# Linear attention and an MLP in one kernel: the attention in sub-chunks of 64 tokens instead of 128

## The chip, the cores and the metric

The kernel runs on one core of one Trainium2 chip. The metric is device time in microseconds (us). The kernel before takes 658.77 us, the median of 3 runs (658.64 to 660.05). Traces come from one profiled execution, whose own time is given with it.

Names: PE is TensorE (PEld its weight loads), DVE VectorE, ACT ScalarE, POOL GpSimd, SP SyncE. All products are in float32; in the records each such matmul stands as two weight loads and two matmul records.

## The reference

B = 4 batches, H = 8 heads, S = 768 tokens, D = 64; per head a decay lam between 0.97 and 0.99.

```python
# Linear attention and an MLP in one kernel: the attention in sub-chunks of 64 tokens instead of 128
intra = (qb @ kb.T * Dmask) @ vb            # Dmask[i, j] = lam ** (i - j) for i >= j, else 0
inter = (qb * lam ** (pos + 1)) @ kv_state
out[block] = intra + inter
kv_state = lam ** 64 * kv_state + (kb * lam ** (63 - pos)).T @ vb
...
x = out as (B*S, H*D)                       # 3072 x 512
h = x @ w_in                                # w_in 512 x 2048
g = h - tanh(h)
result = g @ w_out                          # w_out 2048 x 512
```

The block length does not change the result of the attention: a block of 128 with the mask and the powers of 128 tokens gives the same sum.

## The kernel before

The tokens are worked in 6 groups `g` of 128 tokens of all four batches (512 columns). Heads go in pairs: `p` is the pair (4 of them), `j` the head in it, and head j lies on partitions 64 j to 64 j + 63. Each group goes through the attention, through `h` (the function `up` and its relatives; products split in seven and, from group 3 on, again in seven, in the manner of Strassen), through `g - tanh`, and through `down`, `down_twice` (products with w_out, also split).

The attention of a group comes in two halves of two batches, `bs` = (0, 1) and (2, 3). `attention(g)` (L433) lists the pieces of each half, and the main loop places them between the products by calls of `run`:

- `att_transpose` (L315): q and k to head dimension by token, `qt` and `kt`. In groups 0 and 1 by PE (L328) and ACT (L330); from group 2 on by DVE (L335) from small blocks that SP loads in the right order (`load_blocks`, tiles q_blk and k_blk, seven buffers). `qd` = qt times the powers `fwd` (L334, DVE).
- `att_scores` (L337): `sp` = kt x qt, 16 matmuls per half with 64 rows and 128 columns on half of the array each (L344); then DVE multiplies each of four banks with `mask` into `ss` (L349).
- `att_out` (L394): 16 matmuls state x qd on quarters of the array (L410), 16 of v x ss on halves (L416), all in two banks `op`; ACT copies each bank of 512 columns to `xt` (L420).
- `att_state` (L369): 16 matmuls k x v with the decayed k (L385), in one bank `kv`. In groups 1 and 2 DVE multiplies the state and adds kv (L389, L390); from group 3 on ACT puts the scaled state into the bank first (four copies, L378) and copies the bank back (L392). The last group has no state.
- `att_sums` (L423): sums and differences of xt on DVE, for the split products.

The decay of k (times lam^(127-pos)) is one DVE operation per batch in groups 1 and 2 (`att_decay`, L352, within `att_state`), and 8 ACT copies with a scale per batch from group 3 on (`decays`, L361), spread over the steps of the group before it in the stream (iteration g decays group g + 1).

The order is set in three ways. The loop from L1020 on writes out the order of the pieces: in iteration g, the first half of the attention of g + 1 comes after `every(down(g, 2))` (L1055, the products `plain` of L756), then `down` or `down_twice` number 4, then the transposes of the second half, number 5, its scores, number 6, the rest of the second half, and number 7. For group 1 the list `turns` (L967) does this between the plain products of group 0 (L874), where ACT and DVE also round the weights (L283 to L288) and form sums of them (L259 to L262). `early_pieces` (L1099) does the transposes and scores of half 0 of group g + 2 inside the inner steps (L611) of group g + 1. Instructions wrapped in `tied(...)` or `keep_in_program_order` keep the order in which they are written; others may be moved by the scheduler within their engine's stream. And buffers decide: the PSUM tag "att" is a ring of four banks shared by tp, sp, op, kv and some product banks; the natural k tiles have three buffers, so that the k load of batch 3 waits for the kv of half 0 (`load_natural`, L125), and on SP's queue the next group's q_blk and k_blk stand behind it.

The products fetch their weights by POOL's queue: `wb` from `factors`, `fine` and `fine_in` (L709 to L715) through a ring of eight.

Of the kernel before, what the change touches and what calls it, by code (L numbers as in the profile page):

```python
# [18 lines left out]
BLK = 128  # L19
# [5 lines left out]
def kernel(  # L25
# [69 lines left out]
    mask = const.tile([128, 2, NP, BLK], F32)  # L95
    for j in range(2):
        for p in range(NP):
            h = 2 * p + j
            nc.vector.tensor_tensor_scan(out=mask[:, j, p, :], data0=lam_all[:, h:h + 1].to_broadcast([128, BLK]),
                                         data1=ident, initial=0.0, op0=AL.mult, op1=AL.add)  # L100

    fwd = const.tile([128, NP, BLK], F32)

    def powers():
        for j in range(2):
            tc.keep_in_program_order(nc.vector.tensor_copy(
                fwd[ts(j, 64), :, 0], lam_all.rearrange("s (p j) -> s j p", j=2)[ts(j, 64), j, :]))
        m = 1
        while m < BLK:
            tc.keep_in_program_order(nc.vector.tensor_tensor(  # L110
                fwd[:, :, m:2 * m], fwd[:, :, 0:m], fwd[:, :, m - 1:m].to_broadcast([128, NP, m]), op=AL.mult))
            m *= 2


    bwd = mask.rearrange("s j p i -> s p j i")[:, :, :, BLK - 1:BLK].to_broadcast([128, NP, 2, D])

    lam_blk = fwd[:, :, BLK - 1:BLK][:, None, :, :].to_broadcast([128, 2, NP, D])
# [9 lines left out]
    def load_natural(g, b, names):  # L127
        for name, src, bufs in (("q", q, 2), ("k", k, 3), ("v", v, 4)):
            if name in names:
                x = (qpool if name == "q" else io).tile([128, H, D], F32, name=f"{name}_nat", tag=name, bufs=bufs)  # L130
                op = nc.sync.dma_start(out=x, in_=src[b, :, ts(g, BLK), :].rearrange("h s d -> s h d"))
                tc.keep_in_program_order(op)
                raw[g, b][name] = x
# [12 lines left out]
    def load(n):  # L146

        while at["loaded"] < min(n, len(chunks)):  # L150
            g, b = chunks[at["loaded"]]
            if g < GB:
                raw[g, b] = {}
                load_natural(g, b, "qk")
                for x in (b - 1, b) if b % 2 else ():
                    load_natural(g, x, "v")
                at["loaded"] += 1
                continue
            for b in range(B):
                raw[g, b] = {}  # L160
            nat = "kv" if g < NG - 1 else "v"

            first = (0, 1, 2) if g == GB else ()
            for b in first:
                load_natural(g, b, nat)
            for b in range(B - 1):
                load_blocks(g, b, "qk")
            load_blocks(g, 3, "q")
            for b in (0, 1):
                if b not in first:  # L170
                    load_natural(g, b, nat)
            load_blocks(g, 3, "k")
            for b in (2, 3):
                if b not in first:
                    load_natural(g, b, nat)
            at["loaded"] += B
# [133 lines left out]
    state = const.tile([128, B, NP, D], F32)  # L310
# [4 lines left out]
    def att_transpose(g, bs):  # L315
        for b in bs:
# [15 lines left out]
            if g > 0:  # L332
                qd = work.tile([128, NP, BLK], F32, name="qd", tag="qd")
                nc.vector.tensor_tensor(qd, qt, fwd, op=AL.mult)  # L334
            tr[g, b] = (qt, kt, qd)  # L335

    def att_scores(g, bs):  # L337
        for b in bs:
            qt, kt, _ = tr[g, b]

            sp = [bank("sp", "att", 4).rearrange("s (p i) -> s p i", p=NP) for _ in range(2)]
            for p in range(NP):
                for j in range(2):
                    tied(g != GI, nc.tensor.matmul(out=sp[j][:, p, :], lhsT=kt[ts(j, 64), p, :],  # L344
                                                            rhs=qt[ts(j, 64), p, :], start=p == 0, stop=True,
                                                            skip_group_check=True))
            ss = work.tile([128, 2, NP, BLK], F32, name="ss", tag="ss")
            for j in range(2):
                tied(g == 0, nc.vector.tensor_tensor(ss[:, j], sp[j], mask[:, j], op=AL.mult))  # L349
            sc[g, b] = ss  # L350

    def att_decay(g, b):  # L352
        kp = raw[g, b]["k"].rearrange("s (p j) d -> s p j d", j=2)
        tied(g != 1, nc.vector.tensor_tensor(kp, kp, bwd, op=AL.mult))

    def decays(g, bs):

        for b in bs if g < NG - 1 else ():
            for h in range(H):
                k_h = raw[g, b]["k"][:, h, :]  # L360
                tc.keep_in_program_order(nc.scalar.activation(  # L361
                    k_h, k_h, AF.Copy, scale=mask[:, h % 2, h // 2, BLK - 1:BLK]))
# [6 lines left out]
    def att_state(g, bs):  # L369
        if g == NG - 1:  # L370
            return

        kv = bank("kv", "att", 4).rearrange("d (b p e) -> d b p e", b=2, p=NP)
        st = state[:, bs[0]:bs[0] + 2]
        filled = g > GI
        if filled:
            for p in range(NP):
                nc.scalar.activation(kv[:, :, p], st[:, :, p], AF.Copy, scale=fwd[:, p, BLK - 1:BLK])  # L378
        for n, b in enumerate(bs):
            kd, vn = raw[g, b]["k"], raw[g, b]["v"]  # L380
            if 0 < g <= GI:
                att_decay(g, b)
            for p in range(NP):
                for j in range(2):
                    tied(g == 0, nc.tensor.matmul(out=kv[ts(j, 64), n, p, :], lhsT=kd[:, 2 * p + j, :],  # L385
                                                  rhs=vn[:, 2 * p + j, :], start=not filled and n == 0 and p == 0,
                                                  stop=True, skip_group_check=True))
        if 0 < g <= GI:
            nc.vector.tensor_tensor(st, st, lam_blk, op=AL.mult)  # L389
            nc.vector.tensor_tensor(st, st, kv, op=AL.add)  # L390
        else:
            tied(g == 0, nc.scalar.activation(st, kv, AF.Copy))  # L392

    def att_out(g, bs):  # L394
# [4 lines left out]

        def dst(n, p, j):  # L400
            return ops[p // 2][ts(j if p < 2 else 1 - j, 64), p % 2, n, :]


        if g > 0:
            for n, b in enumerate(bs):
                for p in (0, 1):
                    for j in range(2):
                        r = ts(j, 64)
                        for pp in (p, p + 2):
                            nc.tensor.matmul(out=dst(n, pp, j), lhsT=state[r, b, pp, :], rhs=tr[g, b][2][r, pp, :],  # L410
                                             start=n == 0 and p == 0, stop=False, skip_group_check=True)
        for n, b in enumerate(bs):
            ss, vn = sc.pop((g, b)), raw[g, b]["v"]
            for p in range(NP):
                for j in range(2):
                    tied(g == 0, nc.tensor.matmul(out=dst(n, p, j), lhsT=vn[:, 2 * p + j, :], rhs=ss[:, j, p, :],  # L416
                                                  start=g == 0 and n == 0 and p % 2 == 0,
                                                  stop=n == 1 and p % 2 == 1, skip_group_check=True))
        for x in range(2):
            tied(g == 0, nc.scalar.activation(  # L420
                xt[g, half][:, 2 * x:2 * x + 2, :].rearrange("d p (b s) -> d p b s", b=2), ops[x], AF.Copy))

# [10 lines left out]
    def attention(g):  # L433
        pieces = [[(fn, g, bs) for fn in (att_transpose, att_scores, att_out, att_state)] for bs in ((0, 1), (2, 3))]
# [302 lines left out]
    def down(g, n):  # L737
# [14 lines left out]
        for u in range(NU):  # L752
            wb = piece(g, n, u)
            for m in range(2):
                for kt in range(2):
                    nc.tensor.matmul(out=t[:, m, :], lhsT=a[:, u, kt, ts(m, 128)], rhs=wb[:, kt, :],  # L756
                                     start=first and u == 0 and m == 0 and kt == 0, stop=u == NU - 1 and kt == 1,
                                     skip_group_check=True)
# [42 lines left out]
    def down_twice(g, n, zw):  # L801
# [5 lines left out]
        for x, a, dst, keep in ((1, a11, y, o[:, 0:128]), (2, a12, zw[:, 0:128], None), (6, s2, y, o[:, 128:256]),  # L807
# [3 lines left out]
            for u in range(NU):  # L811
                nc.tensor.matmul(out=dst, lhsT=a[:, u, :], rhs=wb[:, ts(u, 128)], start=x in (1, 2) and u == 0,  # L812
                                 stop=u == NU - 1, skip_group_check=True)
# [50 lines left out]
    def up_plain(u, cs):  # L864
# [5 lines left out]
        for i in range(KI):  # L870
            for c in cs:
                a, t = divmod(c - 11, 10)
                for m in range(2):
                    tied(u == 0, nc.tensor.matmul(  # L874
# [19 lines left out]
    def down_first(kt, ns):  # L894

        u, m = divmod(kt, 2)
        for n in ns:
# [4 lines left out]
            for r in range(2):  # L902
                nc.tensor.matmul(out=acc[n][:, r, :], lhsT=a[:, ts(r, 128)], rhs=b, start=kt == 0 and r == 0,  # L903
                                 stop=kt == KH - 1, skip_group_check=True)
# [29 lines left out]
    for b in (0, 1):  # L934
# [33 lines left out]
             (3, 11, 0, p0[1:2]), (3, 21, 1, p0[2:4]), (2, 12, 1, ()), (2, 22, 1, p1[0:1]), (3, 12, 1, p1[1:2]),  # L968
# [18 lines left out]
    run(p1[2:4])  # L987
    weights(NU * KI + 6)
    run(p1[4:])
    for kt in range(KH):  # L990
        down_first(kt, (1, 2))
        if kt + 1 < KH:
# [27 lines left out]
    for g in range(1, NG):  # L1020
        last = g == NG - 1
        (p0, p1), step = ahead, 0
        for u in range(NU):
            if g < GI:
# [12 lines left out]
                if u > 1:  # L1037
                    run(p0[u - 2:u - 1])
# [14 lines left out]
        if twice(g, 4):  # L1053
            sums_twice(g, 4)
        every(down(g, 2))  # L1055
        run(p0[2:])
        sums_twice(g, 5)
        zw = ("w", "z") if g >= GI else ("z", "w")
        every(down_twice(g, 4, zw[0]) if twice(g, 4) else down(g, 4))
# [14 lines left out]
        run(p1[1:2])  # L1074
# [11 lines left out]
        run(p1[2:])  # L1086
# [4 lines left out]
        every(down_twice(g, 7, zw[1]) if twice(g, 7) else down(g, 7))  # L1091
# [70 lines left out]
```

## Time and profile before

| | |
|---|---|
| median of 3 runs | 658.77 us (658.64 to 660.05) |
| the profiled execution | 658.55 us, span 656.8 us, granted clock 1.00 |
| PE busy | 647.6 us, 99% of the span |
| DVE, ACT, POOL busy | 480.6, 244.3, 234.1 us (73%, 37%, 36%) |
| DMA | 140.68 MB, 214 GB/s on average |
| scores, L344 | 384 records of 279 ns |
| inter L410, intra L416 | 320 records of 275 ns; 384 of 276 ns |
| kv, L385 | 320 records of 223 ns |
| xt L420, decays L361, L378 (ACT) | 24 of 596 ns, 64 of 337 ns, 16 of 370 ns |
| ss L349 (DVE) | 48 of 684 ns |

A record's time is its latency; matmuls overlap, so the length of a block of them is read from the starts, or from the chain of waits, which merges consecutive instructions of one line. A group's line gives: line, engine, operation, output and inputs by the program's names, the part of the array and the shape, the count, then busy us, mean ns, and the idle time of the engine just before with what ended most of it.

### The profile page before, as it was taken

Reading aid. Unit: us, or ns where it says so; the run is one execution under the profiler, and the core shown is the slowest. Engines: PE = TensorE matmul, PEld = TensorE weight load, DVE = VectorE, ACT = ScalarE, POOL = GpSimd, SP = SyncE. Lnnn points to the kernel's source line nnn. Section 1 sums busy time; section 2 is a strip of 40 time slices with the busy share of each in tenths; the row PEclk is TensorE's granted clock in tenths of the full one; section 3 lists DMA queues with packets and bytes.
Section 4 is the critical chain, followed back from the end, with each engine's and each line's share of the span. In section 5 each row is a group of like instructions: output and inputs, shape, how many; then the busy total and the mean of one; then the engine's idle time right before and its main releaser. Section 6 shows DMA issues by size and latency. Waiting matters only on the chain.

```text
span 656.8 us, 13884 instructions
## 1 busy us (share of the span) xinstructions
PE 647.6 (99%) x5160; PEld 596.4 (91%) x5160; DVE 480.6 (73%) x929; ACT 244.3 (37%) x502; POOL 234.1 (36%) x400
## 2 busy tenths in 40 slices
PE   7899999999999999999999999999999999999998
PEld 6788888888888999998999998899998899998897
DVE  4577886745788889569866578987567987457963
ACT  3897825503221111246341235533333322333310
POOL 0000535735432355220454521256411246621261
PEclk9999999999999999999999999999999999999999
DMA  9989988969665898874899877599956277942394
GB/s 211 232 238 246 302 287 232 332 168 256 187 159 145 226 288 259 259 183 111 217 301 278 221 181 200 130 283 269 294 133 149 94 241 249 251 144 66 85 306 155
DMA packets 167699, 140.68 MB, mean 214 GB/s; under 512 B 134800, under 2 KB 137488, under 8 KB 167632
## 3 DMA queue, kind: packets, MB, share of 16 engines
q0 software_dynamic: 33376, 106.19, 51.0%
q1 hardware_dynamic: 134112, 33.59, 25.2%
q8 instruction: 41, 0.67, 0.4%
q14 instruction: 26, 0.21, 0.1%
q10 hardware_dynamic: 144, 0.00, 0.0%
HBM read 111.42 MB, written 28.31 MB: 213 GB/s over the span
## 4 chain that ended last, share of the span: by engine, by line
PE 59%; DMA 1%; issue 1%; POOL 0%; DVE 0%; POOLq 0%
PE plain L756 11%; PE y L611 10%; PE y L812 9%; PE zw L812 7%; PE z L611 5%; PE y L533 4%; PE zs L533 4%; PE w L611 3%; PE sp L344 2%; PE op L416 2%; PE end L858 1%; PE op L410 1%; DMA wb<-fine_in 1%; PE kv L385 1%; POOL wb L709 0%
## 5 line engine op out<-in xcount | busy, mean ns | idle before, releaser
L712 POOL DMA_DIRECT2D wb<-fine x133 | 73.8, 555 | 155.2 <-PE plain L756 103.4
L756 PE MATMUL plain<-wb,g 128*128 128x256 f32 x416 | 94.9, 380 | 0.0
L756 PEld LDWEIGHTS plain<-wb,g 128*128 128x128 f32 x416 | 78.0, 190 | 10.3
L715 POOL DMA_DIRECT2D wb<-factors x64 | 34.5, 540 | 70.9 <-PE z L611 51.1
L874 PE MATMUL h<-xt,w 128*128 128x256 f32 x256 | 57.6, 382 | 2.2 <-DVE w L288 2.0
L815 ACT ACTIVATE q<-y 128x128 f32<-128x128 f32 x76 | 21.1, 278 | 96.5 <-PE y L812 95.1
L874 PEld LDWEIGHTS h<-xt,w 128*128 128x128 f32 x256 | 47.8, 190 | 9.4 <-DVE w L288 2.0
L709 POOL DMA_DIRECT2D wb<-fine_in x60 | 35.6, 625 | 32.0 <-PE y L611 6.5
L812 PE MATMUL y<-wb,g 128*128 128x128 f32 x336 | 44.8, 278 | 0.0
L514 ACT ACTIVATE th<-g 128x512 f32<-128x512 f32 x48 | 29.4, 627 | 34.2 <-DVE g L539 34.0
L812 PEld LDWEIGHTS y<-wb,g 128*128 128x128 f32 x336 | 40.7, 192 | 1.1 <-issue 0.3
L602 ACT ACTIVATE g<-y 128x512 f32<-128x512 f32 x24 | 14.3, 597 | 63.6 <-PE y L611 63.6
L349 DVE TENSOR_TENSOR ss<-sp,mask 128x512 f32<-128x512 f32 x48 | 30.3, 684 | 7.6 <-PE sp L344 7.6
L903 PE MATMUL acc<-wt,g 128*128 128x256 f32 x144 | 32.7, 380 | 0.0
L515 DVE TENSOR_TENSOR g<-g,th 128x512 f32<-128x512 f32 x48 | 31.9, 685 | 0.4
L611 PE MATMUL z<-tt,wb 128*128 128x128 f32 x256 | 31.9, 275 | 0.0
L903 PEld LDWEIGHTS acc<-wt,g 128*128 128x128 f32 x144 | 27.2, 190 | 3.9 <-DVE g L910 0.2
L533 PE MATMUL y<-xt,w 128*128 128x256 f32 x128 | 30.3, 379 | 0.0
L533 PE MATMUL zs<-xt,ws 128*128 128x256 f32 x128 | 30.2, 379 | 0.0
L611 PEld LDWEIGHTS z<-tt,wb 128*128 128x128 f32 x256 | 30.2, 192 | 0.0
L812 PE MATMUL zw<-wb,g 128*128 128x128 f32 x224 | 29.6, 275 | 0.0
L284 ACT ACTIVATE r<-raw 128x512 int16<-128x512 uint32 x32 | 25.1, 784 | 7.0 <-DMA raw<-in_moe_w_out_dram 4.0
(224 smaller groups left out, 1484.0 us busy)
## 6 DMA issues: line engine op xcount, KB each, us to landing
wb<-fine POOLq DMA_DIRECT2D x133, 256.0 KB, 4.0
wb<-factors POOLq DMA_DIRECT2D x64, 256.0 KB, 4.3
wb<-fine_in POOLq DMA_DIRECT2D x60, 256.0 KB, 5.0
v_nat<-in_v_dram SPq DMA_DIRECT2D x24, 256.0 KB, 5.0
raw<-in_moe_w_out_dram POOLq DMA_DIRECT2D x12, 512.0 KB, 5.4
k_nat<-in_k_dram SPq DMA_DIRECT2D x20, 256.0 KB, 4.7
out_dram<-q POOLq DMA_DIRECT2D x20, 256.0 KB, 4.2
fine<-wt POOLq DMA_DIRECT2D x17, 256.0 KB, 4.2
```

Source lines behind the costliest of these rows:

```text
L349: tied(g == 0, nc.vector.tensor_tensor(ss[:, j], sp[j], mask[:, j], op=AL.mult))
L514: tied(held, nc.scalar.activation(th, src, AF.Tanh))
L515: nc.vector.tensor_tensor(dst(c), src, th, op=AL.subtract)
L533: nc.tensor.matmul(out=t[:, m, :], lhsT=wt[:, kt, ts(m, 128)], rhs=x[:, kt, :], start=False, stop=kt == 1, skip_group_check=True)
L611: nc.tensor.matmul(out=dst[:, ts(u, 128)], lhsT=a, rhs=b, start=(x in (1, 5) or x == 2 and not filled) and u == 0, stop=True, skip_group_c ...
L709: nc.gpsimd.dma_start(out=t.rearrange("p m c -> p (m c)"), in_=fine_in[INNER.index(n_[1]), (5, 6, 3).index(x_)].rearrange("p u c -> p (u c)"))
L712: nc.gpsimd.dma_start(out=t.rearrange("p m c -> p (m c)"), in_=fine[TWICE.index(n_), SUB.index(x_)].rearrange("p u c -> p (u c)"))
L715: nc.gpsimd.dma_start(out=t, in_=factors[XAT[FACT[n_][1]]][:, 2 * x_:2 * x_ + 2, :])
L756: nc.tensor.matmul(out=t[:, m, :], lhsT=a[:, u, kt, ts(m, 128)], rhs=wb[:, kt, :], start=first and u == 0 and m == 0 and kt == 0, stop=u = ...
L812: nc.tensor.matmul(out=dst, lhsT=a[:, u, :], rhs=wb[:, ts(u, 128)], start=x in (1, 2) and u == 0, stop=u == NU - 1, skip_group_check=True)
L874: tied(u == 0, nc.tensor.matmul(out=hm[c][:, m, :], lhsT=w1[u][:, i, a, ts(m, 128)], rhs=xt[0, t][:, i, :], start=m == 0 and i == 0, stop= ...
L903: nc.tensor.matmul(out=acc[n][:, r, :], lhsT=a[:, ts(r, 128)], rhs=b, start=kt == 0 and r == 0, stop=kt == KH - 1, skip_group_check=True)
```

## The change

From group 1 on, a group of 128 tokens is worked as two sub-chunks `a` of 64 tokens. Group 0 stays as it was, with masks of its own (`whole`, in the pool of output tiles).

- Scores: only the two diagonal blocks of 64 x 64 are formed, 32 matmuls of 64 x 64 x 64 per half, on four quarters of the array, both batches in two banks; two mask products instead of four.
- kv: 32 matmuls with 64 rows per half (one bank per sub-chunk). In the last group 16, for the first sub-chunk alone, which needs k loads (64 rows) and decays that there were not.
- State: three buffers that rotate, `states(g)` = old, mid, new. mid = lam^64 old (four ACT copies), mid += kv of sub-chunk 0 (DVE), new = lam^64 mid + kv of sub-chunk 1 (four DVE operations).
- Output: `att_inter`, 32 matmuls on quarters into four banks of "att", old for sub-chunk 0 and mid for sub-chunk 1; a small ACT copy `seen` of the last bank; `att_intra`, 32 matmuls on quarters into the same banks; xt in four copies of 256 columns. Between inter and intra stands one step of a product, which `held` ties to the order written.
- Order: `att_state` now comes right after the scores in half 1, and before `down(g, 2)` in half 0 of groups 3 to 5. The decays of groups 1 and 2 move into `att_transpose`. `powers` gets four ACT copies of masks and one step less of `fwd`.

```diff
     def att_scores(g, bs):
+        if g > 0:
+            sp = [bank("sp", "att", 4).rearrange("s (n p i) -> s n p i", n=2, p=NP) for _ in range(2)]
...
+                        for a in range(2):
+                            cols = ts(a, HALF)
+                            tied(g != GI, nc.tensor.matmul(
+                                out=sp[j][ts(a, 64), n, p, :], lhsT=kt[ts(j, 64), p, cols], rhs=qt[ts(j, 64), p, cols],
+                                start=n == 0 and p == 0, stop=True, skip_group_check=True))
...
     def att_state(g, bs):
...
+        old, mid, new = (x[:, pair_] for x in states(g))
+        subs = (0, 1) if g < NG - 1 else (0,)
+        kv = [bank("kv", "att", 4).rearrange("d (b p e) -> d b p e", b=2, p=NP) for _ in subs]
+        for p in range(NP):
+            nc.scalar.activation(mid[:, :, p], old[:, :, p], AF.Copy, scale=fwd[:, p, HALF - 1:HALF])
...
+                    for a in subs:
+                        nc.tensor.matmul(out=kv[a][ts(j, 64), n, p, :], lhsT=kd[ts(a, 64), 2 * p + j, :],
+                                         rhs=vn[ts(a, 64), 2 * p + j, :], start=n == 0 and p == 0, stop=True,
+                                         skip_group_check=True)
+        nc.vector.tensor_tensor(mid, mid, kv[0], op=AL.add)
+        for p in range(NP) if g < NG - 1 else ():
+            nc.vector.scalar_tensor_tensor(out=new[:, :, p], in0=mid[:, :, p], scalar=fwd[:, p, HALF - 1:HALF],
+                                           in1=kv[1][:, :, p], op0=AL.mult, op1=AL.add)
...
+    def att_inter(g, bs):
+        st = states(g)
+        open_[g] = {(x, a): bank("op", "att", 4)[:, 0:256].rearrange("d (p b s) -> d p b s", p=2, b=2)
+                    for a in range(2) for x in range(2)}
...
+                            tc.keep_in_program_order(nc.tensor.matmul(
+                                out=corner(g, x, a, p, n, j), lhsT=st[a][r, b, p + 2 * x, :],
+                                rhs=tr[g, b][2][r, p + 2 * x, ts(a, HALF)], start=n == 0 and p == 0, stop=False,
+                                skip_group_check=True))
+        nc.scalar.activation(seen, open_[g][1, 1][:, :, :, 0], AF.Copy)
+        held["yes"] = True
+
+    def att_intra(g, bs):
+        held["yes"] = False
...
+                            tc.keep_in_program_order(nc.tensor.matmul(
+                                out=corner(g, x, a, p, n, j), lhsT=vn[ts(a, 64), h, :],
+                                rhs=ss[ts(a, 64), j, n, p + 2 * x, :], start=False, stop=n == 1 and p == 1,
+                                skip_group_check=True))
+        for (x, a), t in open_.pop(g).items():
+            nc.scalar.activation(xt[g, half][:, 2 * x:2 * x + 2, :].rearrange("d p (b a s) -> d p a b s", b=2, a=2)[
+                :, :, a], t, AF.Copy)
...
+        if g >= GI:
+            run(p0[2:3])
         every(down(g, 2))
-        run(p0[2:])
+        run(p0[3:4])
         sums_twice(g, 5)
...
+        p4 = down_twice(g, 4, zw[0]) if twice(g, 4) else down(g, 4)
+        next(p4)
+        run(p0[4:])
+        every(p4)
...
-        run(p1[1:2])
+        run(p1[1:3])
...
-        run(p1[2:])
+        run(p1[3:4])
+        p7 = down_twice(g, 7, zw[1]) if twice(g, 7) else down(g, 7)
+        next(p7)
+        run(p1[4:])
```

In the lines of the changed kernel, L431 are the copies for mid, L440 the add to mid, L442 the products for new, L485 is `seen`, L505 the xt copies, L481 inter and L500 intra; its roundings are L291 to L296.

## The prediction

> **What bounds the kernel now.** I read the shares of busy time first, then the slices, the chain that ended last, and the groups by shape.
>
> ```profile
> PE 647.6 (99%) x5160; PEld 596.4 (91%) x5160; DVE 480.6 (73%) x929; ACT 244.3 (37%) x502; POOL 234.1 (36%) x400
> ...
> PE   7899999999999999999999999999999999999998
> ...
> PEclk9999999999999999999999999999999999999999
> ```
>
> PE is busy 99% of the span and in every slice after the second; the granted clock is 1.00 throughout. No other engine has a stage of its own. In the view of waits PE waits 6.2 us in all, almost all of it before 30 us. So time taken out of PE's stream comes off the end, unless PE then waits for something that its own length covers today.
>
> The chain of waits around one half of group 3 shows what the attention costs in that stream:
>
> ```profile
> 310.92 4.96 PE plain L756 x23
> 315.88 1.03 PE op L410 x32
> 316.91 1.90 PE op L416 x32
> 318.81 0.93 PE kv L385 x32
> 319.74 1.09 PE y L812 x8
> ```
>
> Columns: start, length, what. Each float32 matmul is two records (x32 is 16 matmuls). The three blocks take 3.86 us; the scores have a stretch of their own, earlier (273.55, 1.99 us, x32). Groups by shape give the forms:
>
> ```profile
> L344 PE MATMUL sp<-qt,kt 64*128 64x128 f32 x384 | 25.2, 279 | 1.4 <-ACT kt L330 1.4
> L416 PE MATMUL op<-ss,v_nat 128*64 128x128 f32 x384 | 23.6, 276 | 0.0
> L385 PE MATMUL kv<-v_nat,k_nat 128*64 128x64 f32 x320 | 11.3, 223 | 0.2 <-PE op L416 0.2
> L410 PE MATMUL op<-qd,state 64*64 64x128 f32 x320 | 11.0, 275 | 0.0
> ```
>
> 128*64 is the part of the array, 64x128 the moving operand. Only L410 uses quarters today; only L385 has 64 columns.
>
> **Rounds.** In the records' starts, matmuls on different parts of the array begin 7 ns apart and then the next round follows: L344 two tiles each 112 ns, L410 four tiles each 109 ns, both with 128 columns; L385 two tiles each 58.5 ns with 64 columns (16 rounds x 58.5 = 0.94, the 0.93 of the chain). So a round's length goes by its columns, and four tiles fit where two do. What no row shows is four tiles with 64 columns. [...]
>
> **What PE saves.** A new block is 32 matmuls, 64 records, in 16 rounds of four. At L385's round that is 0.94 us; entering and leaving the tile mode costs about 0.29 in L344 (2.08 with its entry, less 16 x 0.112), and L410's first round was some 0.05 longer: I take 0.32, so 1.26 a block. Scores and kv, now side by side, enter once: 2.22. A half costs 2.22 + 2 x 1.26 = 4.74. Before it cost 1.99 + 3.86 and twice 0.09 of entry, 6.03. Saved: 1.29 a half.
>
> Three halves get less. In the new order of PE's instructions the kv of half 0 in groups 3 to 5 is not in one piece: 24 matmuls, a full-array product, 8 more (group 3: scores alone 1.26, kv 1.59, saving 0.66); 24/4/4 in group 4 (0.2); 12/3/1 in group 5, whose kv (first sub-chunk only) is new work: before, a half without kv was 5.10; now it loses 0.84. Half 1 of group 5 wins 0.36. Sum: four halves of groups 1 and 2 5.16; group 3 1.95; group 4 1.49; group 5 -0.48: **8.1 us** off PE. Group 0 is as before.
>
> **What the other engines pay.** DVE: a half's four mask products of 128x512 (684 ns; 0.60 start to start) become two; the two state products (0.68 each) become one add and four small ones (at 0.20 to 0.29 each, by 128x128 rows); DVE is 73% busy and some 3 us shorter in all, at no gain by itself. ACT: four extra mask copies of 64x256 (0.38 estimated between 0.28 for 128x128 and 0.60 for 128x512), four copies of 128x128 with a scale for mid per half (L378: 370 ns, 0.395 apart) where groups 1 and 2 had none, one tiny copy `seen`, xt in four pieces of 256 columns instead of two of 512 (1.09 becomes some 1.5), 32 more decays in group 5 (L361: 337 ns, 0.24 to 0.27 apart, 8 us). ACT is 37% busy, so only its place in the order matters. SP: the q and k copies of the next group stand behind the k load that waits for kv of half 0; that wait now ends some 10 us earlier, so they start earlier; the transposes on DVE that read them come earlier too, but their data was in by about 238 against 239.5. The four extra k loads (64 rows, 128 KB each) go into a queue that no PE wait names after 30 us. I cost both at nothing, up to 3 us (DVE's whole wait for q_blk today).
>
> **New waits on PE**, where the saved time is given back:
>
> 1. Group 1, 57 to 100 us, where DVE and ACT are busiest. Inter needs mid and new, which need kv. Four copies for mid and two of the masks stand in ACT's queue before the roundings (L283 to L285); DVE's L288, which waits for them (it started at 69.67), comes some 1.3 later, about 71.0, and L440 and four L442 stand behind it: 71.0 + 0.6 + 0.6 + 0.33 + 0.2 x 4, less what moves up, is about 72.9. Inter is due at 71.05: 1.8 us. In half 1 the same gives 1.05 (95.05 against 94.0), and transposes that wait for the four xt copies behind roundings give 0.45. Together 3.3; nothing if ACT's idle time (0.80 at 65.37) takes up the shift, 6 if DVE's queue does not move up.
> 2. kv of half 0 in groups 3 to 5 now precedes `down(g, 2)`, seven us of `plain`. It waits for the last decays on ACT:
>
> ```profile
> 308.81 7.07 PE L756 MATMUL plain<-wb,g 128*128 128x256 f32 x32
> ...
> 311.27 1.05 ACT L361 ACTIVATE k_nat<-k_nat,mask 128x64 f32<-128x64 f32 x4
> ```
>
>    The last four end 3.5 us after PE has come to this product (3.8 a group later). The first 24 matmuls and the products between cover all but 0.97, 0.6 and 0.4: 2.0. Ends: 0 if ACT gets there as PE slows, 7 if the pieces wait in turn.
> 3. Intra waits for `seen`. In ACT's queue that stands behind four mid copies (1.6 us), and one of these behind the inter that still reads the buffer; the filler between inter and intra is four y products, 0.89. Some 0.6 is left in three halves (group 3 half 0, group 4 both): 1.8; where the filler is four plain products (1.73) nothing is. Ends: 0 and 4.
>
> Sum of waits 7.1. Covered, as far as I see: new of group 2 half 0 (208.9 against 210.3) and group 3 (317.5 against 318.3); in half 1 6.25 us of products lie between. xt is later by 2 us at most, with 4 to 6 to spare. The profiled run is 658.55 (span 656.8 and 1.75 around it), 0.2 under the median of 658.77. 658.55 - 8.1 + 7.1 = 657.5, and 0.2 for the median: **657.7**.
>
> **Rivals.**
>
> A, the waits do not come: PE's products slide, ACT keeps ahead. 658.77 - 8.1 - 0.8 (two waits of 0.38 for fine_in that the shift may remove) gives 650. For it: ACT is idle 63% of the span. Against: each wait has an instruction named in the new order that stands before it.
>
> B, quarters with 64 columns are not fed fast enough, and the kernel is slower. The new rate is one matmul record per 14.6 ns, each with a weight load. The highest mean rate that any row shows is 27 to 29 ns (L410: 109/4; L385: 58.5/2). The bursts of 7 ns speak against a limit, but a burst may come out of a queue that was filled while the array was busy. At 27 ns a block takes 64 x 0.027 + 0.32 = 2.05, 0.79 more; there are 39 such blocks: +31, less the gain, about 682. The point from which it decides: 1.0 us of waits is left as gain, and 39 blocks x 16 rounds eat it at 1.6 ns more per round; at 20 ns a record it is 658 + 13 = 671. [...]
>
> C, the same mechanisms as in the forecast, but at the upper ends: group 1 at 6, kv at 4 and `seen` at 3 make 13 against 8.1: 663.5.
>
> D, the change does not do what it says: kv pieces split so that nothing is saved in groups 3 to 5, 655 to 658; inside the forecast's range.
>
> **Chances.** Forecast (655 to 661) 0.50, A 0.10, B 0.18, C 0.22. Within the forecast, with 657.7 near the bound, faster 0.5, same 0.28, slower 0.22. A measurement of this kernel tells 0.2% (1.3 us) from no change. Faster: 0.25 + 0.10 + a little of D, 0.37. Same: 0.14 and a little of C, 0.15. Slower: 0.11 + 0.18 + 0.22, less that, 0.48. The range goes from 649.5 (A) to 670 (C and the mild part of B), and leaves the hard form of B out.
>
> **What would show it.** Right: blocks of 64 records lasting 1.2 to 1.3 us; PE gaps near 72, 95, 310 and ahead of intra in groups 3 and 4, summing to some 7 us. B would show as rounds of 100 ns and more, without gaps. A would show 1.26 blocks and none of the gaps. Wrong if DVE, with the smaller products, delays the g tiles that `down` reads, which I cost at nothing.

## The result and the profile after

The changed kernel takes 662.28 us, the median of 5 runs (660.94 to 663.63), against 658.64 us before; the ratio is 1.0053 (95% interval 1.0032 to 1.0075). It is slower by 3.6 us, where no change or a little less (657.7) was forecast. Its profiled execution took 660.94 us (span 659.2), the lowest of the five, so the trace accounts for 2.4 of the 3.6 us. Its mean granted clock is 0.995; of the other four, one has 0.995 (662.28), one 0.997 (662.67) and two 1.000 (661.53 and 663.63).

The page, shares of busy time and granted clock by slices:

```profile
PE 643.5 (98%) x6440; PEld 588.0 (89%) x6440; DVE 477.4 (72%) x946; ACT 260.1 (39%) x588; POOL 234.1 (36%) x400
...
PEclk9999989999999999899999999999999999999999
```

PE is busy for 4.1 us less and the span is 2.4 us longer: PE waits. And the clock row has two 8s that were not there.

The groups by shape, for the four products of the attention:

```profile
L437 PE MATMUL kv<-v_nat,k_nat 64*64 64x64 f32 x576 | 13.3, 220 | 0.9 <-ACT k_nat L404 0.9
L500 PE MATMUL op<-ss,v_nat 64*64 64x64 f32 x640 | 11.9, 221 | 0.3 <-issue 0.3
L481 PE MATMUL op<-qd,state 64*64 64x64 f32 x640 | 11.9, 221 | 0.4 <-DVE state L442 0.4
L362 PE MATMUL sp<-qt,kt 64*64 64x64 f32 x640 | 11.6, 221 | 0.0
```

All of them run on quarters with 64 columns, and each block of 64 records takes 0.98 to 1.09 us by the records' starts where it waits for nothing. The quarters are fed.

The view of waits for PE:

```profile
PE tp L340 <- ACT xt L505: 2.1, 1, 2.1
PE z L696 <- DMA wb<-fine_in: 2.1, 1, 2.1
...
PE kv L437 <- ACT k_nat L404: 0.9, 2, 0.6
PE z L553 <- DVE g L579: 0.7, 1, 0.7
PE op L481 <- DVE state L442: 0.4, 1, 0.4
PE op L500 <- issue: 0.3, 1, 0.3
```

With the lines left out they sum to 12.5 us, 6.3 more than before. Two waits of 2.1 us carry most of it. What followed them is in the view by stretches (columns: stretch, length, busy time of PE, PEld, DVE, ACT, POOL with counts, granted clock, DMA share, GB/s), here 80 to 91 us:

```profile
80.45:83.86 3.41, 1.28 (x9) 0.86 (x8) 0.69 (x1) 3.26 (x10) 1.81 (x3) 1.00 1.10 366
83.86:87.28 3.42, 3.42 (x17) 3.24 (x16) 2.07 (x4) 3.34 (x8) 2.87 (x6) 0.50 1.04 398
87.28:90.69 3.41, 3.41 (x35) 2.77 (x37) 3.34 (x6) 0.22 (x1) 2.39 (x4) 1.00 0.98 322
```

and around the second wait:

```profile
261.35:264.76 3.41, 1.48 (x11) 1.34 (x12) 0.05 (x1) 0.85 (x2) 2.17 (x4) 1.00 0.84 286
264.76:268.18 3.42, 3.42 (x19) 3.42 (x18) 0.69 (x1) 0.56 (x2) 1.09 (x3) 0.50 1.04 365
```

PE is idle for some 2 of 3.41 us, and in the 3.41 us after that the granted clock is 0.50: PE is busy all the time and does half the work (17 records where the next stretch has 35). That is 1.7 us on top of each wait, in this execution. Two of the five executions had a mean granted clock of 1.000, so no whole stretch like this, and were not shorter. Their time went elsewhere, and without a trace of them it stays open where; that their waits were longer is only argued, from the profiles of the experiments below.

All other products are the same 3752 records in the same order in both traces, so the difference of their start times can be split by where it arises (us, after less before; "blocks" are the intervals with attention products in them, waits included):

| stretch of before | blocks | all else |
|---|---|---|
| 60 to 106 (group 1) | -2.42 | +4.23 |
| 180 to 262 (group 2) | -3.62 | +0.20 |
| 262 to 285 (inner products) | -0.89 | +3.73 |
| 285 to 560 (groups 3 to 5) | -1.58 | +1.63 |
| the rest | +0.12 | +0.73 |
| sum | -8.39 | +10.52 |

"All else" holds the wait for xt, the wait for fine_in, the two slow stretches, and 0.10 us for the first record after each way back from a block, which is there more often now.

### The profile page after: what moved, and what is told of

The parts are those of the page before. It is cut to its first block, busy times and chain, and to the rows that moved or that the text cites. A ratio compares the mean times of both kernels' runs of the same rounds, so it can differ in the third digit from the quotient of the medians.

```text
span 659.2 us, 16593 instructions
## 1 busy us (share of the span) xinstructions
PE 643.5 (98%) x6440; PEld 588.0 (89%) x6440; DVE 477.4 (72%) x946; ACT 260.1 (39%) x588; POOL 234.1 (36%) x400
## 4 chain that ended last, share of the span: by engine, by line
PE 65%; DMA 12%; DVE 7%; ACT 7%; SPq 4%; issue 3%; POOL 1%; DVEq 0%; ACTq 0%; POOLq 0%
PE y L696 10%; PE plain L841 9%; PE y L898 8%; PE acc L990 7%; PE zw L898 6%; PE z L696 5%; PE y L618 3%; PE w L696 2%; PE zs L618 2%; DMA wb<-fine_in 2%; SPq L151 2%; DMA raw<-in_moe_w_in_dram 2%; DMA wb<-factors 2%; DMA q_blk<-in_q_dram 2%; PE y L553 2%
## 5 line engine op out<-in xcount | busy, mean ns | idle before, releaser
L841 PE MATMUL plain<-wb,g 128*128 128x256 f32 x416 | 97.3, 383 | 0.2 <-DMA wb<-factors 0.2
L898 PEld LDWEIGHTS zw<-wb,g 128*128 128x128 f32 x224 | 27.2, 192 | 0.3
```

The source lines that it names most:

```text
L841: tied(held["yes"], nc.tensor.matmul(out=t[:, m, :], lhsT=a[:, u, kt, ts(m, 128)], rhs=wb[:, kt, :], start=first and u == 0 and m == 0 and ...
L898: tied(held["yes"], nc.tensor.matmul(out=dst, lhsT=a[:, u, :], rhs=wb[:, ts(u, 128)], start=x in (1, 2) and u == 0, stop=u == NU - 1, skip ...
```

## The experiments

Median, ratio to the kernel before with its interval, and the change against the 662.28 of the changed kernel, whose ratio was 1.0053 (the kernel before had medians of 658.3 to 658.6 beside them):

| kernel | us | ratio | |
|---|---|---|---|
| a_xt_early | 661.30 | 1.0044 (1.0024 to 1.0064) | -1.0 |
| b_write_later | 659.37 | 1.0019 (1.0004 to 1.0035) | -2.9 |
| c_kv_later | 660.38 | 1.0019 (1.0007 to 1.0032) | -1.9 |
| abc_all | 656.71 | 0.9985 (0.9964 to 1.0006) | -5.6 |
| abcd_sums_late | 656.94 | 0.9981 (0.9964 to 0.9998) | -5.3 |
| g1_old_alone | 659.20 | 1.0013 (0.9996 to 1.0030) | -3.1 |
| bc_g1_old | 655.12 | 0.9947 (0.9930 to 0.9964) | -7.2 |
| best_inter_later | 655.07 | 0.9947 (0.9933 to 0.9962) | -7.2 |
| before_wait_9 | 659.42 | 1.0010 (1.0001 to 1.0019) | |
| before_wait_16 | 661.03 | 1.0035 (1.0022 to 1.0049) | |
| before_chain_4 | 662.26 | 1.0058 (1.0043 to 1.0074) | |
| before_chain_12 | 666.48 | 1.0125 (1.0112 to 1.0138) | |

**The wait for xt in group 1.** The order of the changed kernel around it, on PE and ACT:

```profile
76.41 1.16 PE L500 MATMUL op<-ss,v_nat 64*64 64x64 f32 x64
77.50 3.72 PE L961 MATMUL h<-xt,w 128*128 128x256 f32 x16
...
81.72 0.77 ACT L293 ACTIVATE r<-raw 128x512 f16<-128x512 f32 x1
82.35 0.67 ACT L431 ACTIVATE state<-state,fwd 128x128 f32<-128x128 f32 x2
82.92 1.19 ACT L505 ACTIVATE xt<-op 128x256 f32<-128x256 f32 x4
83.34 0.66 PE L340 MATMUL tp<-ident,q_nat 128*128 128x128 f32 x4 [2.13 <-ACT xt L505]
```

Intra was done at 77.5; the copies stand behind roundings on ACT, one of which waited 0.15 us for a DMA, and start at 82.92. op now takes all four banks of the ring, so the transposes of half 1 have no bank until a copy is done. Edit a:

```diff
-        tied(first, nc.scalar.activation(w, hif, AF.Copy, scale=2.0 ** -112))
+        tied(first or ready.get("tie"), nc.scalar.activation(w, hif, AF.Copy, scale=2.0 ** -112))
...
+        ready["tie"] = (g, half) == (1, 0)
...
-            nc.scalar.activation(xt[g, half][:, 2 * x:2 * x + 2, :].rearrange("d p (b a s) -> d p a b s", b=2, a=2)[
-                :, :, a], t, AF.Copy)
+            tied((g, half) == (1, 0), nc.scalar.activation(
+                xt[g, half][:, 2 * x:2 * x + 2, :].rearrange("d p (b a s) -> d p a b s", b=2, a=2)[:, :, a], t, AF.Copy))
```

> The changed kernel with one thing moved: in group 1, half 0, the four xt copies on ACT keep their written place ahead of the later roundings. Theory: the quarters save the time that was worked out, and two waits of 2.1 us on PE, each followed by a stretch of 3.4 us at a granted clock of 0.5 (1.7 us more each), give it back. Here the first of the two, the transposes behind the xt copies at 81 to 83 us, goes and takes its slow stretch along: 662.3 - 3.8 = 658.5. Rival 1, the slow stretch is not the wait's doing: 662.3 - 2.1 = 660.2, and the stretch at 0.5 is still there. Rival 2, a fixed time of the weights at 263 us takes up whatever is gained ahead of it: 662 and a longer wait there.

Measured: 661.3. In its profile the wait for xt is gone and so is the slow stretch behind it (granted clock 1.00 throughout), but inter waits 1.6 us for L442, 1.1 of it in half 0 and 0.5 in half 1, and in half 1 also 0.6 for ss and 0.3 for L440; the changed kernel's inter of half 1 waited for nothing. The stretch 60 to 106 us still costs 1.1 more than before (1.8 in the changed kernel). So a good part of the wait moved on by one step, to the inter of half 1. The wait for fine_in grew too, from 2.1 to 2.4 us, which is rival 2's sign, though small. The size, 3.8, was wrong. Its runs spread from 658.3 to 665.1 and its interval takes in the changed kernel's 1.0053, so a gain from this edit alone is not shown.

The wait is no fixed amount either. Up to 100 us the two kernels of edits b and c, below, have the changed kernel's order on PE, ACT and DVE, and in their profiles this wait is 1.2 and 2.9 us where it was 2.1. In the profile of c, ACT waits 3.18 us for raw weights ahead of the roundings in front of the copies, in that of the changed kernel 0.15 for them.

**The wait for fine_in.** POOL's order in the changed kernel:

```profile
257.19 0.75 POOL L654 DMA_DIRECT2D fine_in<-g  x1 [2.79 <-DVE g L649]
258.37 1.05 PE L696 MATMUL y<-tt,w 128*128 128x128 f32 x8
258.47 3.78 POOL L794 DMA_DIRECT2D wb<-fine_in  x7 [0.53 <-issue]
...
263.28 2.88 PE L696 MATMUL z<-tt,wb 128*128 128x128 f32 x16 [2.07 <-DMA wb<-fine_in]
```

Before, four reads of wb went out first and the last write of fine_in after them:

```profile
257.69 2.19 POOL L709 DMA_DIRECT2D wb<-fine_in  x4 [4.03 <-PE y L611]
...
259.86 0.76 POOL L569 DMA_DIRECT2D fine_in<-g  x1
```

Now the write stands first, waits 2.79 us for DVE's sums and holds up the reads, while PE is earlier by 1.2 us. Edit b ties the write and these reads to the order written:

```diff
-                nc.gpsimd.dma_start(out=fine_in[INNER.index(n)].rearrange("x p u c -> p x (u c)"),
+                tied(n == 6, nc.gpsimd.dma_start(out=fine_in[INNER.index(n)].rearrange("x p u c -> p x (u c)"),
...
-                nc.gpsimd.dma_start(out=t.rearrange("p m c -> p (m c)"), in_=fine_in[
+                tied(g_ == GI and n_[1] != 1, nc.gpsimd.dma_start(out=t.rearrange("p m c -> p (m c)"), in_=fine_in[
```

> The changed kernel with POOL's last write of fine_in put back behind the four reads of wb that the scheduler had let it pass, as in the kernel before. Theory: the wait of 2.1 us at 263 goes with its slow stretch of 1.7: 658.5. Rival 1: 660.2, slow stretch still there. Rival 2, the reads are late in any case since the DMA of this stage is the limit: 662, the wait stays above 1.5 us.

Measured: 659.4, nine tenths of a microsecond short of the theory. In its profile the first read is waited for 0.44 us in place of 2.07, but the three reads behind the write are late in their turn:

```profile
261.15 0.76 POOL L654 DMA_DIRECT2D fine_in<-g  x1
...
266.05 2.02 PE L696 MATMUL y<-tt,wb 128*128 128x128 f32 x16 [1.71 <-DMA wb<-fine_in]
```

No slow stretch follows here. This execution took 661.3, 1.9 above the median, and in it PE waits 0.44 and 1.71, so 2.1 us, for these reads, as long as in the changed kernel; by this profile rival 2's sign, a wait above 1.5 us, is there. The profiles of all versions together speak for the order: the four with the write ahead (the changed kernel, a, c, g1_old_alone) wait 2.1, 2.4, 2.7 and 2.6 us for fine_in, the five with edit b (b, abc_all, abcd_sums_late, bc_g1_old, best_inter_later) 2.1, 0.5, 0.8, 1.3 and 1.9. So the order on POOL's queue is a large part, and something else can make these reads late as well; whether the DMA of this stage is the limit no run shows.

**kv ahead of the plain product.** Edit c:

```diff
-        if g >= GI:
-            run(p0[2:3])
         every(down(g, 2))
-        run(p0[3:4])
+        if g >= GI:
+            run(p0[2:3])
+            held["yes"] = True
+        else:
+            run(p0[3:4])
...
         next(p4)
+        if g >= GI:
+            next(p4)
+            next(p4)
+            run(p0[3:4])
+            next(p4)
         run(p0[4:])
```

> The changed kernel with the kv of half 0 in groups 3 to 5 after the plain product instead of ahead of it, and inter three products later. Theory: kv is one block again and waits for no decays, 1.4 us in group 3, 1.5 in group 4, 0.7 in group 5: 662.3 - 3.6 = 658.7. Rival: xt comes later by three products and the sums or the second half wait for it, or inter waits for the add to mid: 662 to 664.

Measured: 660.4. kv is one block of 1.1 us again, and no wait for k_nat is left; yet half of the gain is missing. In its profile the two waits that this edit leaves alone are longer, 2.9 us for xt and 2.7 for fine_in, each with its slow stretch, and inter waits 2.4 us for L442 in three places. Group 3 of its trace, DVE and PE:

```profile
321.83 0.68 DVE L440 TENSOR_TENSOR state<-state,kv 128x512 f32<-128x512 f32 x1
...
323.03 1.11 DVE L442 SCALAR_TENSOR_TENSOR state<-state,fwd,kv 128x128 f32<-128x128 f32 x4
323.19 0.44 PE L481 MATMUL op<-qd,state 64*64 64x64 f32 x10
...
324.29 1.04 PE L481 MATMUL op<-qd,state 64*64 64x64 f32 x54 [0.66 <-DVE state L442]
```

Inter reads old and mid; mid is done at 322.51 (L440), and still its sixth matmul waits for the end of L442, which writes new. What the two have in common is the bank: L442 reads kv of sub-chunk 1, and op takes that bank too. The fifth matmul reads mid as well and runs; the sixth is the first that writes the last of the four op banks.

All three:

> All three edits in one. Theory: they add up, 662.3 - 3.8 - 3.8 - 3.6 = 651, faster than both kernels. Rival 1 (no slow stretches to win): 654.5. Rival 2 (a wait further on takes up the gain): 656 to 660, with a wait of PE above 1.5 us that none of the three had.

The three gains of the medians add up (1.0 + 2.9 + 1.9 = 5.8; measured 5.6), though to half of what was expected. In its profile inter waits 3.1 us for L442, in four places; PE's wait for fine_in is 0.5. The theory's 651 was missed, and rival 2's 656 to 660 is where it came out, by several waits of at most 1.4 us instead of one above 1.5.

**Group 1.** With b and c, and group 1 back in blocks of 128, whose products take two op banks and one kv bank, in the order of before (banks, order and the products themselves go back together here, so this run doesn't tell them apart):

```diff
     def att_scores(g, bs):
-        if g > 0:
+        if g > 1:
...
+        if g == 1:
+            kv = bank("kv", "att", 4).rearrange("d (b p e) -> d b p e", b=2, p=NP)
...
+            nc.vector.tensor_tensor(new, old, lam_blk, op=AL.mult)
+            nc.vector.tensor_tensor(new, new, kv, op=AL.add)
+            return
...
+        fns = (att_transpose, att_scores, att_out, att_state) if g == 1 else (
+            att_transpose, att_scores, att_state, att_inter, att_intra)
```

> Edits b and c, and group 1 back in blocks of 128 tokens (scores, state and products as before; sub-chunks from group 2 on, with two more DVE operations for the powers up to 128). Theory: in the profile of abc_all the stretch from 60 to 106 us costs 2.6 us more than in the kernel before, in spite of what the quarters save there, since the four op banks take the whole ring and DVE and ACT are full; without it 656.7 - 2.6 = 654.1. Rival: the wait for fine_in at 263 takes it up, as its reads do not come earlier: 656 to 657.

Measured: 655.1, faster than both kernels by more than the interval. Group 1's stretch is back to the time of before to within 0.01 us; in the rest the blocks save 7.1 us and all else gives back 3.1.

The same edit of group 1 without b and c:

> The changed kernel with group 1 alone back in blocks of 128 tokens; edits b and c not made. Theory: the stretch of group 1 (60 to 106 us) cost 1.8 us net in the changed kernel's profile, its slow stretch included; the wait at 263 and the kv pieces of groups 3 to 5 stay: 660.5, with PE's wait for fine_in still near 2 us. Rival (most of the loss is group 1's): 658.6 or less.

Measured: 659.2, between the changed kernel and bc_g1_old, and between the theory's 660.5 and the rival's 658.6. In its profile the wait for fine_in is 2.6 us, with a slow stretch after it (mean granted clock 0.997).

DVE's sums out of the way, on top of abc_all:

```diff
-            if u == 2:
-                sums_in(0)
...
+        if (u, c) == (3, 12):
+            sums_in(0)
```

> abc_all, and DVE's four sums of the first weights (sums_in(0)) after the scores and kv of group 1, half 1, instead of ahead of them. Theory: inter of that half waits 1.0 us for the last product for new, since its four banks include the two of kv, and these four sums (2.4 us) stand ahead of that on DVE; the wait goes: 655.7, or 654.5 where it had led to a slow stretch. Rival: the sums are then late for their own readers or DVE's order hardly changes: 656.7.

Measured: 656.9, no gain over 656.7. Inter still waits 3.6 us for L442 in its profile, in four places, so the place of these sums was not what held L442 up.

Inter five products after kv, on top of bc_g1_old:

```diff
-            next(p4)
-            next(p4)
+            for _ in range(4):
+                next(p4)
             run(p0[3:4])
             next(p4)
```

> bc_g1_old with inter of half 0 in groups 3 to 5 five products after kv instead of three. Theory: in c_kv_later inter comes 1.0 to 1.2 us too early, since its four banks include the two of kv and wait for the last product for new; two products more (1.8 us) cover that in three halves: 655.1 - 2 = 653. Rival: xt, now 1.8 us later, is late for the sums or its banks are late for the scores of half 1: 655 or more.

Measured: 655.07 against 655.12: no gain. The waits of inter for L442 are gone from the view of waits, and the blocks now save 9.1 us, but PE waits 1.9 us for fine_in and 1.4 us for fine. Its profiled execution, 656.88, is the longest of the six. The theory was right about the wait and wrong that nothing stood behind it.

**Does a wait slow the clock?** The first attempt put a bank with copies ahead of the scores:

```diff
+        t = bank("hold", "att", 4)
+        tc.keep_in_program_order(nc.tensor.matmul(out=t[:, 0:128], lhsT=ident, rhs=ident, start=True, stop=True))
+        for _ in range(n):
+            tc.keep_in_program_order(nc.scalar.activation(t[:, 0:128], t[:, 0:128], AF.Copy))
```

> The kernel before, with nothing changed but a wait put into PE's stream in group 4: ahead of the scores of half 1 a small product goes into a bank of the ring and ACT copies 128 columns of it onto itself 9 times; the fourth bank of the scores is that bank. Estimate from L815's 278 ns: 9 copies take some 2.4 us, of which 1.1 are covered, a wait of some 1.2 us. Theory (a wait that leaves a fixed stretch of 3.4 us less than about half idle costs only itself): 658.6 + 1.2 = 659.8, granted clock 1.00. Rival: any wait above some 1 us slows the clock: 661.5.

> The same with 16 copies: a wait of some 3 us. Theory: where 1.9 us or more of it fall into one of the fixed stretches of 3.4 us, the next stretch is granted 0.5 and costs 1.7 more: 658.6 + 3 + 1.7 = 663.3 in most executions, 661.6 in the others. Rival: slow stretches are not the waits' doing: 661.6 always, granted clock 1.00.

The wait did not come about: in both profiles the scores run while the copies go on. The two say nothing on the question. (before_wait_16 does not form the reference's result, so its row is no time of this kernel at all.) The second attempt makes PE read the end of the chain:

```diff
+        tc.keep_in_program_order(nc.scalar.activation(chain, t[:, 0:128], AF.Copy))
+        for _ in range(n - 1):
+            tc.keep_in_program_order(nc.scalar.activation(chain, chain, AF.Copy))
+        tc.keep_in_program_order(nc.tensor.matmul(out=t[:, 0:128], lhsT=chain, rhs=ident, start=True, stop=True))
```

> The kernel before with a wait that PE cannot pass: in group 4 ahead of the scores of half 1 a small product (128 columns), 4 ACT copies of 128x128 in a chain (278 ns each by L815's rows, behind up to 1 us of decays), and a second small product that reads the last copy; one product of 0.45 us stands in between. A wait of some 1.5 us. Theory: less than about 1.9 us of wait in one stretch of 3.4 us costs itself alone: 660.3, granted clock 1.00. Rival: 662, with a slow stretch after it.

> The same with 12 copies: a wait of some 3.8 us. Theory: at least one stretch of 3.4 us has 1.9 us of it or nearly so, and the next is granted 0.5: 658.6 + 3.8 + 1.7 = 664.1, with the slow stretch right behind the wait in the profile. Rival: the slow stretches have nothing to do with waits: 662.4, granted clock 1.00 around the wait.

With 12 copies the wait is 5.0 us. By stretches, cut where the clock changes:

```profile
438.01:441.42 3.41, 0.00 (x0) 0.00 (x0) 0.00 (x0) 3.09 (x12) 0.00 (x0) 1.00 0.81 210
441.42:444.84 3.42, 2.87 (x14) 2.67 (x16) 0.00 (x0) 0.52 (x2) 0.52 (x1) 0.50 0.23 36
444.84:448.25 3.41, 3.41 (x33) 3.19 (x31) 1.34 (x3) 0.00 (x0) 0.02 (x1) 0.50 0.52 112
448.25:451.66 3.41, 3.41 (x31) 3.41 (x32) 2.45 (x4) 0.55 (x2) 1.33 (x3) 1.00 0.40 71
```

Two stretches at 0.50, 6.83 us, cost 3.4: 5.0 + 3.4 = 8.4, and the medians differ by 8.2 (666.48 against 658.29). That settles it for a whole stretch without work. The second slow stretch comes behind one that was itself slow and busy for 2.87 us only; behind the slow stretches of the changed kernel, which were busy throughout, the clock was back at 1.00. With 4 copies the wait is 2.3 us and falls on a border:

```profile
434.59:438.00 3.41, 1.98 (x18) 1.78 (x16) 2.28 (x5) 2.65 (x12) 1.61 (x3) 1.00 1.05 330
438.00:441.42 3.42, 2.58 (x35) 2.34 (x36) 0.97 (x2) 0.72 (x3) 0.00 (x0) 1.00 0.66 173
```

1.44 and 0.83 us idle, and no slow stretch; that execution took 661.14 us. The other three took 661.56, 663.38 and 662.96, at granted clocks of 1.000, 0.997 and 0.999. One slow stretch in 660 us makes 0.997, so the second had one, which would fit its 1.8 to 2.2 us more than the two at 1.000. Where it lay can't be seen without a trace, and executions of the kernel before with 0.997 took 658.6 to 659.1, hardly more than the rest. The third had no whole slow stretch and was nearly as long. So why these two are longer stays open.

## Why the prediction was wrong, point by point

- **What PE saves: right.** 8.1 us was forecast, 8.4 is what the blocks lost with the waits inside them. 1.26 us a block was 1.09 to the next record, with 0.09 more in front (309 ns from the record before, where 216 are usual) and 0.10 behind: 1.28. That the totals agree so well is partly luck: group 2 saved 3.62 where 2.58 was forecast, groups 3 to 5 2.47 where 2.96 was. Rival B, the quarters not being fed, fell: a round of four takes what kv's round of two took, 64 records in about 1 us, some 16 ns each.
- **The sum of the waits: nearly right, for wrong reasons.** 7.1 forecast, 6.3 measured, of other parts. Group 1: the inter of half 0 waited some 0.6 and not 1.8, that of half 1 not at all; the transposes waited 2.1 and not 0.45. The kv of half 0: 0.9 as a wait against 2.0. Intra behind `seen`: about 0.6, in group 4 half 1 alone, against 1.8.
- **The step that failed first: "two waits of 0.38 for fine_in that the shift may remove".** This stands in rival A alone; the sum of the forecast left these waits as they were. The reading was off too: the view of waits of before has one wait of PE for fine_in after 30 us, of 0.2 us (0.38 by the records' starts). I let PE's gain of group 2 stand and left POOL's order unread. The write had moved ahead of four reads, and PE's wait for fine_in went from 0.2 to 2.1. By the medians edit b is worth 2.9 us.
- **The step that failed beside it: a wait priced at its own length.** In the profiled execution both waits of 2.1 us had a slow stretch of 3.4 us at half clock behind them, 3.4 us together, which no term of the sum held. Taken off its 660.94, they leave 657.5, what the sum gave for a profiled run; that it fits so closely is luck, since the waits were other ones. The profile of before could not show it, as no PE wait there after 31 us is above 0.4 us. For the median it is not the whole reason: two executions without a slow stretch took 661.53 and 663.63.
- **Group 1's cause was half seen.** I named ACT's queue, and in item 1 a wait of 0.45 for the xt copies, but not that op now holds the whole ring of four banks, so that tp waits for xt, and inter for L442. 0.45 became 2.1 here, and 1.2 and 2.9 in two profiles of the same order. That the gain was to be had elsewhere shows in bc_g1_old.
- **Rivals A and C.** A fell: the waits came. C's 663.5 is near the 662.28, but by luck: it had 13 us of waits, 6 of them in group 1, 4 before kv and 3 behind `seen`, where the profile shows 6.3 in all, 0.9 before kv and 0.6 behind `seen`.
- **The size of my theories after the result.** a was expected at 3.8 and gave 1.0, c 3.6 and 1.9: the next wait stood 1 to 2 us behind the one removed, and the waits that were left alone differed from execution to execution.

What stays open: what the executions of the changed kernel without a slow stretch lost their time to; what limits the fetches of `fine` and `fine_in` in the fastest versions (PE waits 3.3 us for them in best_inter_later).

## What to carry to other kernels

On a PE that is busy 99% of the span, count first which banks and queue places the faster form takes: a step that needs the whole ring can turn a late copy into a PE wait (1.2 to 2.9 us for xt here). Read the new order of each DMA queue too, not only of the compute engines. And price a PE wait of about 2 us or more at its length and up to 1.7 us more: here six waits of 2.1 to 5.0 us had a slow stretch of 3.4 us or more at a granted clock of 0.50 behind them, while those of 2.4 us (a_xt_early) and 2.3 us (before_chain_4) had none. Look at the granted clock of every execution as well: one profile need not tell where the median's time went.

## What the runs showed of the hardware

In the changed kernel's trace the two stretches at 0.50 begin 180.9 us apart, 53 times 3.413 us, and each lasts 3.413 us; in that of c_kv_later they begin 180.9 us apart as well (85.13 and 266.04), and in that of the kernel before the two changes of the granted clock, at the start and at the end, are 651.9 us apart, 191 times 3.413. So in these traces the granted clock went by stretches of 3.413 us on a fixed beat. A slow stretch began behind stretches in which PE was idle for 1.9 and 2.1 us (the changed kernel), 2.7 and 2.9 us (c_kv_later) and 3.4 us (before_chain_12), and once behind 1.4 us (abc_all, 93.21 to 96.62); none began behind 1.7 us in a_xt_early, 1.7 us in b_write_later and 1.4 us in before_chain_4. So of these nine, all five with 1.9 us or more in one stretch were followed by one, and of the four with 1.4 to 1.7 us one. The second slow stretch of before_chain_12 stands apart: it came behind a slow one that was idle for 0.5 us. By where a wait fell it cost 1.7 us more or not: 2.1 us in the changed kernel had a slow stretch behind it; 2.4 us in a_xt_early and 2.3 us in before_chain_4, each over a border, had none. The spread of the changed kernel's five runs is not explained by this, as the shortest (660.94) had two slow stretches and the longest (663.63, granted clock 1.000) none. On quarters with 64 columns, 64 matmul records took 0.98 us in the changed kernel, some 15 ns from start to start.
